# An mLSTM cell followed by a hash-routed MoE layer: places of two q transposes, the first division and the middle gates' rows, and of the first expert's weight loads

## The chip, the cores and the metric

The kernel runs on one core of one Trainium2 chip. The metric is device time in microseconds (us) of one execution; less is better. Nine runs of the kernel before gave a median of 353.56 us (352.61 to 356.6). One execution of it was profiled.

## The reference

Four batches of eight heads, 768 time steps, head dimension 40. Per head a recurrence keeps a 40x40 matrix C and a vector n; the output row of each step is gated and becomes one row of x (3072 tokens of 320 numbers). Each token then goes to one of eight experts, chosen by a hash of its id.

```python
for t in range(S):
    m_new = np.maximum(f[t] + m, i[t])
    f_stab, i_stab = np.exp(f[t] + m - m_new), np.exp(i[t] - m_new); m = m_new
    C = f_stab * C + i_stab * einsum('bhd,bhe->bhde', v[t], k[t])
    n = f_stab * n + i_stab * k[t]
    y[t] = sigmoid(o[t]) * (C @ q[t]) / np.maximum(np.abs(n @ q[t]), 1.0)
x = y.transpose(0, 2, 1, 3).reshape(B * S, H * D)
expert = token_ids * 2654435761 % 8
for e in range(8):
    out[expert == e] = np.maximum(x[expert == e] @ w1[e], 0) @ w2[e]
```

## The kernel before

**Two parts.** The first part computes the recurrence in chunks of 128 time steps: 24 steps s = 0 to 23, four batches (b = s % 4) times six chunks (c = s // 4). The second part is the MoE: expert 0 with rows turned early, then experts 1 to 7.

**A step of the first part.** Each engine takes its instructions in the order in which the program writes them; nothing reorders them, and an instruction that waits holds up all behind it on its engine. Step s writes this on TensorE: `turn(s+2)` (L382: four transposes of k and four of q into the two PSUM buffers of tag `tr`, each copied out to kT or qT by ScalarE, L395), `scores(s+1)` (L441: k times q), `decays(s+1)` (L397: products of the tiles L and R, which hold the gates' rows, exponentiated by ScalarE into w, L414), `state(s)` (L469: the chunk's sum for C), `attend(s)` (L490). VectorE does `weigh(s+1)` (L450: scores times w) and `divided(s-1)` (L510: four operations, the last, L518, reads the PSUM tile xh; xh has two buffers, so `state(s)`, which writes a part of the tile of step s+1, needs `divided(s-1)` done). GpSimd does `k_weights` (L426), `decayed` and `gated`.

**The gates.** Three groups: g0 for chunk 0, g1 for the four middle chunks (128 rows: four chunks times 32 heads), g2 for the last. g1 takes f from tile f1 and i from tile i1, both loaded by `middle` (L288); `sums` (L347) makes A, an exponential makes X, `ends` (L364) makes e, `split` (L355) and `rows` (L360) cut each into three bf16 parts in the tile zt1. From there they go through DRAM: `keep_a` (L271, rows A and X) and `keep_e` (L274, rows e) write them out, and `load_a(s)` (L243, into one of three R tiles) and `load_e(c)` (L252, into one of two L tiles) read them back in the layout that `decays` needs. A read waits for the end of the write of the same DRAM tensor. `load_a(4)` and `load_e(1)` are the first to read g1, and `decays(4)`, in step 3, the first to use them. `weights` (L369) makes kwT1 for `k_weights`: an exponential on ScalarE, a transpose on TensorE (L374), a copy on VectorE.

**The queue.** Nearly all loads are issued by SyncE (SP), in program order: per step k and q of step s+5, v of step s+4 (160 KB each, six buffers each), the gates' rows, o_gate, and stores of finished x rows up to step 16. Before the steps L279 to L808 write the start: loads of the first k, q, v, the gates of g0, `turn(0)` to `turn(2)`, and so on. The last steps' stores, the gathers of x rows by expert and the scatters are on GpSimd's queue.

**The first expert's weights** are loaded by pieces in the steps (`slices_of`, L120): w1 in two pieces of 512 KB (steps 17, 18), its last 64 rows w1c (step 19), w2 in four pieces of 320 KB (steps 20 to 23). In step 20 two gathers fetch expert 0's first 256 rows (L881); `early_turn(0)` and `early_turn(1)` (L744) transpose them in steps 22 and 23, the second ahead of `attend(23)`. After `attend(23)`, `layer1` of expert 0 runs (L901).

Of the kernel before, what the change touches and what calls it, by code (L numbers as in the profile page):

```python
# [8 lines left out]
F32 = mybir.dt.float32  # L9
# [8 lines left out]
P = 128  # L18
# [4 lines left out]
def kernel(  # L23
# [24 lines left out]
    nc = tc.nc  # L48
# [5 lines left out]
    E, _, F = moe_w1.shape  # L54
# [65 lines left out]
    def slices_of(e):  # L120

        w1t = wpools[0].tile([P, 2, F], F32, name="w1t")
        w1c = wpools[0].tile([P, FB // 2, P], F32, name="w1c")
        w2t = w2pools[0].tile([P, FB, Dm], F32, name="w2t")
        W[e] = w1t, w1c, w2t
        last = moe_w1[e][2 * P :, :].rearrange("d (a two f) -> two d a f", two=2, f=P)
        rows = moe_w2[e].rearrange("(a p) d -> p a d", p=P)

        def part(i):
            if i < 2:  # L130
                nc.sync.dma_start(w1t[:, i], moe_w1[e][i * P : (i + 1) * P, :])
            elif i == 2:
                for j in range(2):
                    nc.sync.dma_start(w1c[j * P // 2 : (j + 1) * P // 2], last[j])
            else:
                r = slice(2 * (i - 3), 2 * (i - 2))
                nc.sync.dma_start(w2t[:, r], rows[:, r])

        return [lambda i=i: part(i) for i in range(7)]

    def layer1(w, xT, h, c0, c1, bank):

# [47 lines left out]
    with tc.tile_pool(name="gates", bufs=1) as gp, \  # L190
# [61 lines left out]
        def load_e(c):  # L252
            g, r = pieces_of(c)
            nc.sync.dma_start(
                Ls[c % 2][: 3 * H], ze[g][r : r + BH].rearrange("(b h) (i t) -> (h i) b t", h=H, i=3),
            )
# [14 lines left out]
        def keep_a(g, zt, n, eng):  # L271
            eng.dma_start(zx[g][:n].rearrange("i r t -> r i t"), zt[:, :n])

        def keep_e(g, zt, eng):  # L274
            eng.dma_start(ze[g], zt[:, 6:9].rearrange("r i t -> r (i t)"))
# [12 lines left out]
        def middle(t, src):  # L288
            nc.sync.dma_start(t[:], src[:, P : S - P].rearrange("r (c t) -> c r t", t=P))

        middle(f1, flat[0])
        load(2, "k")

        ind = gp.tile([3 * H, H], F32, name="ind")
# [41 lines left out]
        class Gates:  # L336
# [32 lines left out]
            def weights(self, dst, tag="tr"):  # L369
                nc.scalar.activation(  # L370
                    self.a[:], self.t["e"][:, 0], AF.Exp, bias=self.t["A"][:, 0, P - 1 : P],
                )
                tp = ps.tile([P, self.n], F32, name="tpg", tag=tag, bufs=2)
                nc.tensor.transpose(tp[:], self.a[:], ident[: self.n, : self.n])  # L374
                nc.vector.tensor_copy(dst[:], tp[:])

# [5 lines left out]
        def turn(s, what, tag="tr"):  # L382
            turned_in(s, what, tag)
            turned_out(s, what)
# [65 lines left out]
        def weigh(s):  # L450
            d = st[s]
            for hf in range(2):
                nc.vector.tensor_tensor(d["w"][:, hf], d["sp"][hf][:], d["w"][:, hf], op=ALU.mult)  # L453
# [278 lines left out]
        for i in range(8):  # L732
            pieces.setdefault(12 + i, []).append(lambda i=i: route_hot(i))
            if i % 2:
                products[12 + i] = [lambda i=i // 2: route_table(i)]
        for i, part in enumerate(slices_of(0)):
            pieces.setdefault(17 + i, []).append(part)
        gates_of = {}
        for i, j in enumerate((4, 5, 6, 6, 7, 8, 8, 9)):
            gates_of.setdefault(j, []).append(i)  # L740
# [27 lines left out]
        load(0, "v")  # L768
        load(2, "q")
        keep_e(0, g0.zt, nc.sync)  # L770
        nc.vector.tensor_tensor_scan(m_sb[:, 1:], f_sb[:], i_sb[:], NEG, op0=ALU.add, op1=ALU.max)
        unread(6)
        turn(0, "k")
# [19 lines left out]
        middle(i1, flat[1])  # L793
        decays(0)
        turn(2, "k")
        load(1, "v")
        load(3, "k")
        load(3, "q")
        weigh(0)
        nc.vector.tensor_copy(Rs[2][:], Rs[0][:])  # L800
        turn(2, "q")
        load_e0()
        load_a(2)
        load(2, "v")
# [5 lines left out]
        for s in range(NT):  # L810
            b, c = place(s)
            if s + 3 < NT and s not in (1, 2):
                load_a(s + 3)
            if s + KV - 1 < NT:
                load(s + KV - 1, "k")
                load(s + KV - 1, "q")
            if s == 1:
                load_a(4)
                load_e(1)
            if s + KV - 2 < NT:  # L820
                load(s + KV - 2, "v")
            if b == 0 and 0 < c < NB - 1:
                load_e(c + 1)
            if s == 2:
                load_a(5)
            for i in gates_of.get(s + 2, ()) if s + 2 < NT - 1 else gates_of[NT - 1] if s == NT - 3 else ():
                load(i, "o")
            if s == 2:
                nc.sync.dma_start(tok[:], moe_token_ids.rearrange("(b c p) -> c b p", b=B, c=NB))
            if s == 13:  # L830
                keep_a(2, g2.zt, 6, nc.sync)
                keep_e(2, g2.zt, nc.sync)
            for i in waiting.pop(s, []):
                store(i)
            decayed(s)
            if s > 0:
                divided(s - 1)
            if s + 2 < NT:
                if s > 0:
                    turn(s + 2, "k")  # L840
                    turn(s + 2, "q")
            if s == 4:
                nc.scalar.activation(g2.t["X"][:, 0], g2.t["A"][:, 0], AF.Exp)
            if s in (7, 10, 12):
                g2.rows({7: "A", 10: "X", 12: "e"}[s], nc.scalar.copy)
            for piece in pieces.get(s, []):
                piece()
            if s + 1 < NT:
                scores(s + 1)
            if s + 1 < NT:  # L850
                k_weights(s + 1)
                decays(s + 1)
            if s == 0:
                nc.scalar.activation(g1.t["X"][:, 0], g1.t["A"][:, 0], AF.Exp)
            state(s)
            if s + 1 < NT:
                weigh(s + 1)
            if s == 0:
                g1.split("A")
                g1.rows("A", nc.scalar.copy)  # L860
                g1.split("X")
                g1.rows("X", nc.scalar.copy)
                g1.ends()
                g1.split("e")
                g1.rows("e", nc.scalar.copy)
                keep_a(1, g1.zt, 6, nc.sync)
                keep_e(1, g1.zt, nc.sync)
                ends_rows(Ls[1])
                nc.gpsimd.tensor_copy(Lx[:], one[:, 1].to_broadcast([P, HB]))
            for i in gates_of.get(s, ()):  # L870
                gate(i)
                if i < s:
                    gated(i)
                    if i < LS:
                        waiting.setdefault(s + 1, []).append(i)
                    else:
# [375 lines left out]
```

## Time and profile before

| what | value |
|---|---|
| median of nine runs | 353.56 us |
| the profiled execution's own time | 353.06 us |
| its span (first to last instruction) | 351.3 us |
| outside the span | 1.76 us |
| TensorE (PE) busy | 334.7 us, 95% of the span |
| VectorE / ScalarE / GpSimd busy | 229.7 / 138.9 / 214.5 us |
| clock granted to TensorE in the run | 0.993 |
| DMA moved | 59.18 MB, 168 GB/s over the span |

How to read it: a timeline line has the start in us, the duration, the engine, the line of the kernel, the operation, output and inputs, the number of instructions merged, and in square brackets the idle time of the engine just before it with what ended that. PE is TensorE's matrix multiply, DVE VectorE, ACT ScalarE, POOL GpSimd, SPq the issuing of DMAs by SyncE: such a line's time is the time that the issue held the queue, not that of the transfer. A wait for several things is put down to the one that came last by the profile, which can be a coincidence. Beside the instructions the trace has a record of each completion count that a transfer gives; eight counters are used in turn by the transfers of SP and ACT, so that each landing can be matched to its transfer by order.

### The profile page before, as it was taken

What the parts mean: (1) busy time and instruction counts of PE and PEld (TensorE: products, weight loads), DVE (VectorE), ACT (ScalarE), POOL (GpSimd) and SP (SyncE); (2) the same over time, 40 slices, a digit from 0 to 9 for tenths busy, and PEclk for the clock granted to TensorE, in tenths of its full rate; (3) what the DMA queues carried; (4) which work ended last, traced back from release to release, by engine and by line L of the source; (5) the groups of instructions that cost most, each with busy time, mean ns of one, the idle gap of its engine ahead of it and who ended that gap; (6) DMA issues with size and microseconds to landing.
All of it is one profiled execution on the core that took longest, in us unless ns stands there. A gap on an engine that the chain in (4) does not pass through costs nothing.

```text
span 351.3 us, 9214 instructions
## 1 busy us (share of the span) xinstructions
PE 334.7 (95%) x3573; PEld 291.9 (83%) x3573; DVE 229.7 (65%) x512; ACT 138.9 (40%) x325; POOL 214.5 (61%) x301
## 2 busy tenths in 40 slices
PE   7889999999999989999999999999999999999990
PEld 5677888888888866788899899789899899899860
DVE  8867897998887841156765886925766856844510
ACT  5676688776766631111412312311512412313300
POOL 8832778989886547408718938816917828526521
PEclk9999999999999999999999999999999999999997
DMA  6699999999999933699968869586486592010010
GB/s 130 121 196 184 162 193 192 209 189 199 190 215 229 258 114 104 175 242 284 236 206 241 283 105 336 145 235 205 115 218 223 113 281 93 0 38 19 18 40 1
DMA packets 162358, 59.18 MB, mean 168 GB/s; under 512 B 140171, under 2 KB 158119, under 8 KB 162313
## 3 DMA queue, kind: packets, MB, share of 16 engines
q1 hardware_dynamic: 158377, 49.05, 59.5%
q0 software_dynamic: 2832, 9.34, 7.9%
q8 instruction: 29, 0.48, 0.6%
q10 hardware_dynamic: 1104, 0.18, 0.3%
q14 instruction: 16, 0.13, 0.1%
HBM read 46.48 MB, written 12.38 MB: 168 GB/s over the span
## 4 chain that ended last, share of the span: by engine, by line
PE 75%; DMA 6%; issue 5%; DVE 4%; SPq 4%; POOL 2%; ACT 1%; ACTq 0%; POOLq 0%; DVEq 0%
PE mh L991 20%; PE mh L1075 14%; PE mh L1042 9%; PE mh L999 6%; PE sp L447 6%; PE tr L390 5%; PE xh L505 5%; PE xh L499 3%; DMA xg<-x_rows,g_idx 3%; PE ab L405 3%; PE xh L478 2%; SPq L1137 2%; DMA w1t<-in_moe_w_dram 1%; SPq L237 1%; PE mh L1155 1%
## 5 line engine op out<-in xcount | busy, mean ns | idle before, releaser
L917 POOL DMA_INDIRECT out_dram<-zo,s_idx x26 | 26.7, 1029 | 69.3 <-issue 47.2
L1042 PE MATMUL mh<-w2t,h 128*128 128x320 f32 x160 | 45.0, 433 | 0.5 <-ACT h L166 0.5
L1042 PEld LDWEIGHTS mh<-w2t,h 128*128 128x128 f32 x160 | 30.0, 190 | 11.8 <-ACT h L166 0.9
L977 DVE TENSOR_TENSOR h<-u,mh 128x416 f32<-128x416 f32 (+1 forms) x56 | 25.5, 475 | 16.6 <-PE mh L999 7.8
L505 PE MATMUL xh<-v,w 128*64 128x41 f32 x768 | 34.6, 222 | 0.0
L453 DVE TENSOR_TENSOR w<-sp,w 128x512 f32<-128x512 f32 x48 | 30.8, 682 | 3.5 <-ACT w L414 3.5
L414 ACT ACTIVATE w<-ab 128x512 f32<-128x512 f32 x48 | 26.2, 596 | 16.8 <-PE ab L405 15.9
L991 PE MATMUL mh<-tx,sw 128*128 128x208 f32 x168 | 31.9, 340 | 0.5 <-DVE sw L947 0.5
L505 PEld LDWEIGHTS xh<-v,w 128*64 128x64 f32 x768 | 30.6, 138 | 0.0
L991 PEld LDWEIGHTS mh<-tx,sw 128*128 128x128 f32 x168 | 29.7, 190 | 0.8 <-DVE sw L947 0.8
L447 PE MATMUL sp<-qT,kT 64*128 64x128 f32 x384 | 28.5, 285 | 1.2 <-ACT qT L395 1.0
L110 POOL DMA_INDIRECT xg<-x_rows,g_idx x24 | 23.3, 972 | 9.0 <-issue 6.4
L977 DVE TENSOR_TENSOR u<-m,mh 128x416 f32<-128x416 f32 x28 | 16.5, 588 | 18.7 <-PE mh L991 17.9
L447 PEld LDWEIGHTS sp<-qT,kT 64*128 64x128 f32 x384 | 23.8, 187 | 5.3 <-issue 3.1
L1075 PE MATMUL mh<-tw,sh 128*128 128x160 f32 x168 | 27.4, 299 | 0.0
L499 PE MATMUL xh<-C,qs 128*64 128x82 f32 x320 | 27.3, 249 | 0.0
L522 POOL TENSOR_TENSOR x<-x,og 128x320 f32<-128x320 f32 x24 | 20.6, 864 | 7.9 <-ACT og L439 4.8
L1075 PEld LDWEIGHTS mh<-tw,sh 128*128 128x128 f32 x168 | 24.3, 190 | 0.0
L991 PE MATMUL mh<-xT,w1t 128*128 128x208 f32 x112 | 23.1, 339 | 0.0
L488 POOL TENSOR_TENSOR C<-C,add 64x164 f32<-64x164 f32 x32 | 16.1, 503 | 10.2 <-ACT add L482 8.9
L1005 ACT COPY m<-mh 128x416 f32<-128x416 f32 x14 | 7.1, 505 | 37.9 <-PE mh L991 37.9
L913 ACT COPY zo<-mh 128x320 f32<-128x320 f32 x12 | 5.1, 425 | 42.6 <-PE mh L1042 27.3
(241 smaller groups left out, 778.8 us busy)
## 6 DMA issues: line engine op xcount, KB each, us to landing
w2t<-in_moe_w_dram SPq DMA_DIRECT2D x7, 1280.0 KB
w1t<-in_moe_w_dram SPq DMA_DIRECT2D x7, 1024.0 KB
xb<-x_slots SPq DMA_DIRECT2D x84, 52.0 KB
k<-in_k_dram SPq DMA_DIRECT2D x24, 160.0 KB
v<-in_v_dram SPq DMA_DIRECT2D x24, 160.0 KB
og<-in_o_gate_dram SPq DMA_DIRECT2D x24, 160.0 KB
q<-in_q_dram SPq DMA_DIRECT2D x23, 160.0 KB
x_slots<-xg SPq DMA_DIRECT2D x7, 480.0 KB
```

The costliest lines, as they stand in the source:

```text
L110: nc.gpsimd.indirect_dma_start(out=xg, out_offset=None, in_=x_d[:rows, :], in_offset=bass.IndirectOffsetOnAxis(ap=idx, axis=0),)
L414: nc.scalar.activation(w[:, hf], ab[:], AF.Exp)
L447: nc.tensor.matmul(sp[hf][:, j, :], lhsT=d["kT"][r, j, :], rhs=d["qT"][r, j, :], start=True, stop=True)
L453: nc.vector.tensor_tensor(d["w"][:, hf], d["sp"][hf][:], d["w"][:, hf], op=ALU.mult)
L499: nc.tensor.matmul(xh[t, 2 * j : 2 * j + 2, :], lhsT=d["qs"][:, j, t], rhs=Cs[b][c % 2][:, j].rearrange("p h d -> p (h d)"), start=True, s ...
L505: nc.tensor.matmul(hs[t, 2 * j + hf, :], lhsT=d["w"][:, hf, j, t], rhs=d["v"][:, 2 * j + hf, :], start=(c == 0), stop=True, skip_group_che ...
L917: ins = nc.gpsimd.indirect_dma_start(out=out[:, :], out_offset=bass.IndirectOffsetOnAxis(ap=idx, axis=0), in_=zo[:], in_offset=None, bound ...
L977: nc.vector.tensor_tensor(o, a, b, op=ALU.add)
L991: nc.tensor.matmul(pair(bank[n])[:, a], lhsT=lhsT(g + a), rhs=rhs, start=first and a == 0, stop=True, skip_group_check=True,)
L999: nc.tensor.matmul(pair(bank[n])[:, a], lhsT=w1c[k, g + a, :], rhs=xT[k, 2, r], start=False, stop=True, skip_group_check=True,)
L1042: nc.tensor.matmul(zp, lhsT=h[:, fb, j * P : (j + 1) * P], rhs=w[2][:, fb, :], start=(fb == 0), stop=(fb == FB - 1),)
L1075: nc.tensor.matmul(bank[n], lhsT=lhsT(f), rhs=rhs(f), start=first and f == 0, stop=f == FB // 2 - 1, skip_group_check=True,)
```

## The change

In the start: `middle(f1)` goes from its place ahead of `load(2, "k")` to the place behind `keep_e(0)`; `load(1, "v")` goes behind the loads of k and q of step 3; `turn(2, "q")` goes into step 0, behind `attend(0)`. In step 0, `keep_a(1)` comes ahead of the loads of k, q of step 5 and v of step 4; `attend(0)`, `turn(2, "q")` and `divided(0)` come ahead of g1's `ends` and `split("e")`. g1's rows e, `keep_e(1)` and `load_e(1)` go into step 1, behind `decays(2)` and behind step 1's loads. The exponential of kwT1 goes from step 2 to step 1 (behind `attend(1)`), its transpose and copy stay in step 2. Expert 0's w1 is loaded in four pieces of 256 KB (each half of the columns of one block of 128 rows): two in step 19, two in step 21; w1c in step 20; all of w2 in step 22. No arithmetic is added or removed.

```diff
@@ slices_of
-            if i < 2:
-                nc.sync.dma_start(w1t[:, i], moe_w1[e][i * P : (i + 1) * P, :])
-            elif i == 2:
+            if i < 4:
+                f = slice(i // 2 * F // 2, (i // 2 + 1) * F // 2)
+                nc.sync.dma_start(w1t[:, i % 2, f], moe_w1[e][i % 2 * P : (i % 2 + 1) * P, f])
+            elif i == 4:
...
-        return [lambda i=i: part(i) for i in range(7)]
+        return [lambda i=i: part(i) for i in (0, 1, 4, 2, 3, 5, 6, 7, 8)]
@@ the start
-        middle(f1, flat[0])
         load(2, "k")
...
         keep_e(0, g0.zt, nc.sync)
+        middle(f1, flat[0])
...
         middle(i1, flat[1])
         decays(0)
         turn(2, "k")
-        load(1, "v")
         load(3, "k")
         load(3, "q")
+        load(1, "v")
         weigh(0)
         nc.vector.tensor_copy(Rs[2][:], Rs[0][:])
-        turn(2, "q")
@@ pieces
-        for i, part in enumerate(slices_of(0)):
-            pieces.setdefault(17 + i, []).append(part)
+        for s, part in zip((19, 19, 20, 21, 21, 22, 22, 22, 22), slices_of(0)):
+            pieces.setdefault(s, []).append(part)
@@ the steps
+            def fetched():
+                if s + KV - 1 < NT:
+                    load(s + KV - 1, "k")
+                    load(s + KV - 1, "q")
+                if s + KV - 2 < NT:
+                    load(s + KV - 2, "v")
...
             if s == 1:
                 load_a(4)
-                load_e(1)
-            if s + KV - 2 < NT:
-                load(s + KV - 2, "v")
+            if s > 0:
+                fetched()
...
-            if s > 0:
+            if s > 1:
                 divided(s - 1)
...
                 decays(s + 1)
+            if s == 1:
+                g1.rows("e", nc.scalar.copy)
+                keep_e(1, g1.zt, nc.sync)
+                load_e(1)
             if s == 0:
                 nc.scalar.activation(g1.t["X"][:, 0], g1.t["A"][:, 0], AF.Exp)
             state(s)
...
                 g1.rows("X", nc.scalar.copy)
+                keep_a(1, g1.zt, 6, nc.sync)
+                attend(0)
+                turn(2, "q")
+                divided(0)
                 g1.ends()
                 g1.split("e")
-                g1.rows("e", nc.scalar.copy)
-                keep_a(1, g1.zt, 6, nc.sync)
-                keep_e(1, g1.zt, nc.sync)
+                fetched()
...
-            attend(s)
+            if s > 0:
+                attend(s)
...
+            if s == 1:
+                g1.exponents()
             if s == 2:
-                g1.weights(kwT1)
+                g1.exponents_turned(kwT1)
```

More of the change, by code (lines that the diff above doesn't have):

```diff
@@ L135, in part @@
             else:
-                r = slice(2 * (i - 3), 2 * (i - 2))
+                r = slice(2 * (i - 5), 2 * (i - 4))
                 nc.sync.dma_start(w2t[:, r], rows[:, r])
-        return [lambda i=i: part(i) for i in range(7)]
+        return [lambda i=i: part(i) for i in (0, 1, 4, 2, 3, 5, 6, 7, 8)]
     def layer1(w, xT, h, c0, c1, bank):
@@ L367, in ends, with weights, exponents @@
                 nc.vector.tensor_sub(e[:, 0], e[:, 0], self.t["A"][:, 0])
-            def weights(self, dst, tag="tr"):
+            def weights(self, dst):
+                self.exponents()
+                self.exponents_turned(dst)
+            def exponents(self):
                 nc.scalar.activation(
@@ L372, in weights, with exponents_turned @@
                 )
-                tp = ps.tile([P, self.n], F32, name="tpg", tag=tag, bufs=2)
+            def exponents_turned(self, dst):
+                tp = ps.tile([P, self.n], F32, name="tpg", tag="tr", bufs=2)
                 nc.tensor.transpose(tp[:], self.a[:], ident[: self.n, : self.n])
@@ L813 @@
                 load_a(s + 3)
-            if s + KV - 1 < NT:
-                load(s + KV - 1, "k")
-                load(s + KV - 1, "q")
+            def fetched():
[4 more added lines that the diff above has]
+                    load(s + KV - 2, "v")
             if s == 1:
                 load_a(4)
-                load_e(1)
-            if s + KV - 2 < NT:
-                load(s + KV - 2, "v")
+            if s > 0:
+                fetched()
             if b == 0 and 0 < c < NB - 1:
```

## The prediction

> **What bounds the kernel now.** I read the page first, then each engine's timeline from 11 to 31 us, then the chain of waits and TensorE's timeline from 104 to 162 us. The page's slices:
>
> ```profile
> PE   7889999999999989999999999999999999999990
> DMA  6699999999999933699968869586486592010010
> ```
>
> TensorE (PE) is full from about 30 us on (in stretches of 5 us it shows 5.00 us from 35 to 115 us). What the first steps gain or lose there passes to the end of the first part unshortened, as no idle time is left that could take it in. So the first steps are read in single stalls. TensorE's timeline:
>
> ```profile
> 12.95 0.63 PE L390 MATMUL tr<-ident,q 128*128 128x128 f32 x4 [0.68 <-DMA q<-in_q_dram]
> ...
> 17.40 0.63 PE L390 MATMUL tr<-ident,q 128*128 128x128 f32 x4 [0.21 <-DMA q<-in_q_dram]
> ...
> 20.49 0.67 PE L478 MATMUL xh<-v,kw 128*64 128x41 f32 x16 [0.83 <-DMA v<-in_v_dram]
> ...
> 26.61 0.33 PE L374 MATMUL tpg<-ident,a_zt 128*128 128x128 f32 x1 [0.47 <-ACT a_zt L370]
> ...
> 29.00 0.62 PE L405 MATMUL ab<-R,L 128*64 128x512 bf16 x4
> ```
>
> Four stalls sum to 0.68 + 0.21 + 0.83 + 0.47 = 2.19 us: q of step 2, q of step 3, `state(1)`, kwT1. The last line is `decays(4)`, first user of g1's rows; no idle time is noted, so rows and L came in time. The stall of `state(1)` is put down to a v load, but v of step 1 was issued at 12.39 us and by the completion records landed at 15.85 us. VectorE's timeline names the true cause: L518 of `divided(0)` ends at 19.75 + 0.49 = 20.24 us, just ahead of 20.49.
>
> ```profile
> 13.95 0.69 DVE L349 TENSOR_TENSOR a_zt<-f,m 128x128 f32<-128x128 f32 x1
> ...
> 15.68 1.29 DVE L453 TENSOR_TENSOR w<-sp,w 128x512 f32<-128x512 f32 x2 [0.25 <-ACT w L414]
> ...
> 19.75 0.49 DVE L518 TENSOR_TENSOR x<-xh,den 128x320 f32<-128x320 f32 x1
> ```
>
> ScalarE's (rows A, X, e of g1, then kT of step 3):
>
> ```profile
> 17.52 0.51 ACT L362 COPY zt<-A_zt 128x384 bf16<-128x384 bf16 x1 [0.72 <-DVE A_zt L358]
> 18.11 0.51 ACT L362 COPY zt<-X_zt 128x384 bf16<-128x384 bf16 x1
> 19.23 0.51 ACT L362 COPY zt<-e_zt 128x384 bf16<-128x384 bf16 x1 [0.61 <-DVE e_zt L358]
> 19.77 0.58 ACT L395 COPY kT<-tr 128x512 f32<-128x512 f32 x1
> ```
>
> SP's (load of i1, `keep_a`, `keep_e`, `load_a(4)`, `load_e(1)`):
>
> ```profile
> 11.74 0.61 SPq L289 DMA_DIRECT2D i<-in_i_gate_dram  x1
> ...
> 21.05 0.75 SPq L272 DMA_DIRECT2D gate_rows<-zt  x1
> 21.91 0.49 SPq L275 DMA_DIRECT2D gate_ends<-zt  x1
> ...
> 25.17 0.29 SPq L248 DMA_DIRECT2D R<-gate_rows  x1
> 25.55 0.32 SPq L254 DMA_DIRECT2D L<-gate_ends  x1
> ```
>
> A write to DRAM and the read behind it lie 25.17 - 21.05 = 4.12 and 25.55 - 21.91 = 3.64 us apart. At the end of the first part one stall counts:
>
> ```profile
> 125.29 0.52 PE L747 MATMUL tpx<-ident,xg 128*128 128x128 f32 x3 [1.19 <-DMA xg<-x_rows,g_idx]
> ```
>
> The second gather, issued at 119.33 us, takes 5.82 us beside the w2 loads.
>
> **The first steps, part one: the chain through ScalarE.** All times below are of the profiled execution. `turn(2, "q")` leaves its place, with its stall of 0.68 and its 0.63 us. But `scores(1)` behind it writes single PSUM buffers that `weigh(0)` reads until 11.68 + 1.36 = 13.04 us, so it moves from 13.51 to about 13.1, no further: 0.4 us to gain.
>
> `middle(f1)` comes on SP at 11.3. I take i1's row: 0.61 us of issue, and by the completion records landed at 15.25, 3.51 after its issue began; f1 then lands at 11.34 + 3.51 = 14.85, `sums` can start at 14.9 instead of 13.95, and its three operations (0.32, 0.33, 0.42 by the rows of L350 and L353, the first without the overlap that makes it 0.69) end at 15.97. `weigh(1)` starts at 16.05 instead of 15.68: +0.35. Bounds: 0, if f1 lands by 14.5 (the f1 load of before landed 2.72 us after its issue's end by the completion records, which would be 14.67 here), and +0.9, all of 14.85 - 13.95. The rows of A and X follow at the same distances, so rows X end at 18.62 + 0.35 = 18.97.
>
> Here is what I hold to be the new stall. In the changed order the copy of qT(2) is queued on ScalarE behind rows A and rows X, which wait for VectorE. It ends one copy later (0.5 us, L395 by its spacing), at about 19.5. `turn(3, "q")` needs the PSUM buffer that it frees, and `scores(2)` needs qT(2) itself; behind them wait all of TensorE's step 1. So `turn(3, "q")` starts at 19.5 instead of 17.40. From there to `state(1)` the rows of before have 19.66 - 17.40 = 2.26 us without the stall: 21.76 instead of 20.49, +1.27. `divided(0)` is 1.12 us long (19.12 to 20.24) and now stands behind the split of X: done by about 18.4 + 1.1 = 19.5, no wait. So 0.68, 0.21 and 0.83 go, and what is late next costs all of it and 1.27 more. Rows e now stand behind w(2) on ScalarE (about 22.9), and the exponential of kwT1 behind C(1), about 24.5, two and a half us ahead of its transpose: the 0.47 goes. **Sum of part one: +1.27 - 0.47 = +0.80**, `decays(4)` ready at 29.80. Bounds: +0.05 (f1 in time, and `decays(1)` at 14.2, 0.4 sooner: `turn(3, "q")` at 18.75, `state(1)` at 21.0) to +1.35 (f1's +0.9 in place of 0.35).
>
> [...]
>
> **Part two: the round trip of rows e.** SP's order up to v of step 3 has the same transfers plus f1 (+0.65), so `load_a(3)` ends at 19.01 + 0.65 = 19.66 and `keep_a(1)` starts at 19.7 (its rows are ready at 18.97). k, q, v behind it (1.90 us, 19.05 to 20.95 before) end at 22.4. `load_a(4)` waits for `keep_a`'s landing. The rows' distance is 4.12; the shortest store-and-read of the trace is the last x store on GpSimd, 129.97 to the gather's 132.10: 2.13. I take the middle, 3.1: 22.8. It and k, q, v of step 1 take 0.35 + 0.45 + 0.6 + 0.7 = 2.1, plus 0.25 for a queue that is full at times: `keep_e` starts at 25.2, instead of 21.91. Its landing, 2.13 to 3.64 later, I take at 2.9: `load_e(1)` at 28.1 instead of 25.55. By the completion records it landed 2.1 after its issue began: 30.2. `decays(4)` wants it at 29.8: **+0.4**. Bounds: 0 (22.5 + 2.1 + 2.13 + 2.1 = 28.8) to +3.8 (23.8, a k issue that is held as at 22.48 for 1.61 us, 3.64, and 2.88 as q of step 2 took: 33.6). In the wait SP holds back k, q, v of steps 6 and 7 and o_gate; k of step 7 was issued at 26.41 and wanted at 36.6, so that is covered.
>
> [...]
>
> **Part three: w1 and w2.** Bytes and issues stay (one issue of 0.42 us becomes two, twice). From 101.5 to 120 us SP issues without a pause, at up to 3.72 us for w1c's two: the queue is held by transfers, not by dependencies. Another order then ends at about the same time, and the w2 pieces still lie beside the gather of 119.33. I take 0. Bounds: -1.19 (the gather lands in time) and +0.6 (one more w2 piece ahead of the gather, priced by the 0.57 us that a w2 issue took at 114.93). Late weights cost nothing at first: w1's second half is wanted at about 131, w2 at 137.5, the last issue was at 120.0.
>
> **Sum.** +0.80 + 0.4 + 0 = +1.2 against 353.06: **354.3 us**. The median of the nine runs is 0.5 above the profiled execution; the forecast lies 0.7 above that median.
>
> **Rivals.**
> 1. *All four stalls go* and no new one comes: rows A and X are out before TensorE gets to `turn(3, "q")`, `load_e(1)` lands by 28. For it: each edit has the place of one stall. Against: ScalarE's order above. 353.06 - 2.19 = 350.9; with the gather's 1.19, 349.7.
> 2. *Slower: `load_e(1)` is late.* Place: `decays(4)`. With the rows' own distances, 23.8 + 2.1 = 25.9, + 3.64 = 29.55, + 2.1 = 31.65: 1.85 after 29.8; with part one, +2.65: 355.7, and up to 357.7 at 33.6. It decides from the point where `keep_e` lands after 27.7. For it: both distances are measured with fewer loads ahead of `keep_e`. Against: 2.13 was seen too.
> 3. *The gather's stall goes* while the start costs 1.2: 353.06 + 1.2 - 1.19 = 353.1.
> 4. *The first part's shift doesn't reach the end*, since the second part starts from a chain of gathers and loads (119 to 157 us): 353.06. Against: that chain starts from `attend(23)`'s rows, so it shifts too.
>
> **How the numbers follow.** Chances: forecast 0.35, rival 1 0.18, rival 2 0.27, rival 3 0.15, rival 4 0.05. Half a per cent is 1.77 us, about what a measurement can tell from no change: below 351.8 counts as faster (0.18), above 355.3 as slower (0.27), the rest 0.55. The forecast's own range is 353.1 (part one at its low end) to 355.3. The range takes in rival 1 without the gather, 350.9, and rival 2 up to 356.2; left out are some 0.05 below and 0.1 above.
>
> **What would show it.** In the changed profile: TensorE idle for about 1.5 us ahead of `turn(3, "q")` with ScalarE's qT copy as releaser; none ahead of L374; `decays(4)` waiting for L, by 0 to 2 us; 1.2 us idle still ahead of the second `early_turn`. I am wrong if rows X end by 18, if `load_e(1)` is issued by 26.5, or if the gather takes under 4.5 us.

## The result, and the profile after

The changed kernel took 356.06 us in the median of 19 runs (354.92 to 359.52), the kernel before 353.09 us in 62 runs beside it (352.27 to 356.6): a ratio of 1.0097 [1.0077, 1.0117], slower by 0.8 to 1.2%. The forecast was 354.3 us and "about no change". The profiled execution of the changed kernel took 358.67 us (span 356.9), so it is one of the longer ones; 5.6 us lie between its span and that of before. Here and below a ratio leaves out executions more than 1.5% above the fastest of their kernel and has an interval of its own, so it can differ from the quotient of the medians beside it.

The page, slices of 8.9 us (PE and DMA in tenths busy, PEclk the granted clock in tenths):

```profile
PE   7987999999999979999999999999999999999990
PEclk9898999999999999999999999999999999999996
DMA  6688999999899973679887959587477493000010
```

TensorE is full from 37 us on, as before from 30 us. New are the two 8s among the first slices of the PEclk row, which was all 9 up to its last slice before. TensorE's timeline of the first steps and of the second `early_turn` (the bracket is the idle time ahead of the line and what ended it; line numbers are those of the changed kernel: `turn` L396, `decays` L411, `state` L484, the transpose of kwT1 L380, `early_turn` L753):

```profile
19.84 0.66 PE L396 MATMUL tr<-ident,q 128*128 128x128 f32 x4 [1.17 <-ACT qT L401]
...
21.98 0.61 PE L484 MATMUL xh<-v,kw 128*64 128x41 f32 x16
...
27.50 0.33 PE L380 MATMUL tpg<-ident,a_zt 128*128 128x128 f32 x1
...
31.97 0.62 PE L411 MATMUL ab<-R,L 128*64 128x512 bf16 x4 [2.01 <-DMA L<-gate_ends]
...
34.55 1.11 PE L396 MATMUL tr<-ident,k 128*128 128x128 f32 x4
35.46 1.06 PE L396 MATMUL tr<-ident,q 128*128 128x128 f32 x4
...
130.52 0.52 PE L753 MATMUL tpx<-ident,xg 128*128 128x128 f32 x3 [2.33 <-ACT og L445]
```

The old stalls of q, of `state(1)` and of kwT1 are gone. In their place stand 1.17 us ahead of `turn(3, "q")`, 2.01 us for L ahead of `decays(4)`, and transposes that take 1.1 us instead of 0.6: half speed. The second `early_turn` waits 2.33 us. The profile names ScalarE there, but VectorE's copy of the gathered rows, which comes first, itself waits for the gather:

```profile
130.41 0.20 DVE L903 COPY xg<-xg 128x64 f32<-128x64 f32 x1 [2.60 <-DMA xg<-x_rows,g_idx]
```

SP's timeline (the second number is how long the issue held the queue): v of steps 1 and 2, `load_a(3)`, `keep_a(1)`, `load_a(4)`, k of step 6, `keep_e(1)`, `load_e(1)`.

```profile
14.49 1.40 SPq L238 DMA_DIRECT2D v<-in_v_dram  x1
...
16.95 1.03 SPq L238 DMA_DIRECT2D v<-in_v_dram  x1
...
20.15 1.49 SPq L249 DMA_DIRECT2D R<-gate_rows  x1
21.73 0.37 SPq L273 DMA_DIRECT2D gate_rows<-zt  x1
...
24.11 0.84 SPq L249 DMA_DIRECT2D R<-gate_rows  x1
25.05 1.15 SPq L238 DMA_DIRECT2D k<-in_k_dram  x1
...
27.60 0.86 SPq L276 DMA_DIRECT2D gate_ends<-zt  x1
30.37 0.32 SPq L255 DMA_DIRECT2D L<-gate_ends  x1
```

The write of rows e starts 5.7 us later than before (27.60 against 21.91), and the read of L 4.8 us later (30.37 against 25.55).

Added up against the profile of before: `scores(4)` is 0.9 us late (28.80 against 27.91), the wait for L adds 2.0, the half clock 1.5 (`decays(5)` at 37.76 against 33.26, 4.5 late in all), and 0.4 come back by `decays(6)` (42.76 against 38.65). The gather adds 1.1, and 0.35 are lost in the second part.

**The half clock.** The trace records the granted clock. In the profiles of this study it changes between full and half speed at steps of 3.41 us. TensorE's busy time (second number), and the granted clock (third number from the end), in two such windows of the changed kernel:

```profile
30.25:33.66 3.41, 1.69 (x40) 1.41 (x42) 0.81 (x2) 1.17 (x4) 0.00 (x0) 0.98 0.63 113
33.66:37.08 3.42, 3.42 (x33) 3.01 (x32) 3.25 (x10) 1.62 (x5) 1.41 (x2) 0.52 0.85 158
```

The edges of these rows lie 0.12 us too late, hence 0.98 and 0.52 instead of full and half; the half clock lasted from 33.54 to 36.95. In the window ahead of it, 30.13 to 33.54, the wait for L leaves TensorE idle for 1.84 us, and the window at half speed costs it up to another 1.7 us of work (an estimate, half of 3.41). So this wait of 2.01 us is paid nearly twice, with the 1.5 us that the half clock adds above.

### The profile page after: what moved, and what is told of

It reads as the page before. It is cut to its first block, busy times and chain, and to the rows that moved or that the text cites. A ratio compares the mean times of both kernels' runs of the same rounds, so it can differ in the third digit from the quotient of the medians.

```text
span 356.9 us, 9212 instructions
## 1 busy us (share of the span) xinstructions
PE 337.9 (95%) x3573; PEld 295.7 (83%) x3573; DVE 228.5 (64%) x512; ACT 139.2 (39%) x325; POOL 214.5 (60%) x301
## 4 chain that ended last, share of the span: by engine, by line
PE 75%; DMA 6%; issue 5%; DVE 4%; SPq 3%; ACT 2%; POOL 2%; ACTq 0%; POOLq 0%; DVEq 0%
PE mh L1010 20%; PE mh L1094 13%; PE mh L1061 8%; PE sp L453 7%; PE mh L1018 6%; PE tr L396 5%; PE xh L511 4%; PE ab L411 3%; PE xh L505 3%; PE xh L484 2%; SPq L1156 2%; DMA w1t<-in_moe_w_dram 1%; DVE w L459 1%; PE mh L1174 1%; DMA xg<-x_rows,g_idx 1%
## 5 line engine op out<-in xcount | busy, mean ns | idle before, releaser
L453 PE MATMUL sp<-qT,kT 64*128 64x128 f32 x384 | 30.0, 291 | 1.4 <-ACT qT L401 0.8
L453 PEld LDWEIGHTS sp<-qT,kT 64*128 64x128 f32 x384 | 25.0, 193 | 5.8 <-issue 3.0
```

Source lines behind the costliest of these rows:

```text
L453: nc.tensor.matmul(sp[hf][:, j, :], lhsT=d["kT"][r, j, :], rhs=d["qT"][r, j, :], start=True, stop=True)
```

## The experiments

Ratios are to the kernel before, timed on the same chip in the same comparison, with 95% intervals. The study went over several chips. On the one of experiments 1 to 4 the kernel before took 353.63 us, about as in the result; on those of the later ones 355.66 (5 to 8), 356.21 (9 to 12), 355.69 (13 to 16) and 356.19 us (17 and 18). Experiment 11 shows what is different there.

### The parts apart

**1. The order of w1 and w2 alone**, in the kernel before.

```diff
-        for i, part in enumerate(slices_of(0)):
-            pieces.setdefault(17 + i, []).append(part)
+        for s, part in zip((19, 19, 20, 21, 21, 22, 22, 22, 22), slices_of(0)):
+            pieces.setdefault(s, []).append(part)
```

> The kernel before with the new order and pieces of expert 0's weights alone. Theory W (w1's second half and all of w2 now lie beside the two gathers and hold up the second early turn): about +1.0 us against the kernel before, with the second early turn idle for about 2.3 us ahead of it instead of 1.19. Rival (the order of the weight loads has no price; the 1.1 us that the changed kernel shows there come from its late first steps): within 0.3 us, idle 1.2 us.

354.67 us, ratio 1.0020 [1.000, 1.004]: a loss of 0 to 1.4 us. The median rose by the 1.0 us that theory W expected, but not by the wait it named: the second `early_turn` waits 0.66 us in its profile, less than the 1.19 of before.

**2. The start alone**: the changed kernel with the old order of w1 and w2.

> The changed kernel with expert 0's weights loaded as before: the first steps' edits alone. Theory L (load_e(1) reaches decays(4) 2.0 us late, and the waits let TensorE's clock drop): +2.0 to +2.5 us against the kernel before, decays(4) idle for about 2 us, the second early turn for about 1.2. Rival (the weights' order carries the loss): within 0.5 us of the kernel before.

355.2 us, 1.0042 [1.0024, 1.006]: 1.6 us above the kernel before, short of theory L and over its rival. Its profile has the wait for qT and none for L:

```profile
20.25 0.66 PE L395 MATMUL tr<-ident,q 128*128 128x128 f32 x4 [1.66 <-ACT qT L400]
...
30.30 0.62 PE L410 MATMUL ab<-R,L 128*64 128x512 bf16 x4
```

In this execution `keep_e(1)` was issued at 26.13 us, 1.5 sooner than in the changed kernel's profile, though the first steps began later. Where L lands thus differs by more than a microsecond between executions. The two parts sum to 0.6%, the whole costs 1.0%; the intervals are too wide to say whether the parts simply add.

**3. The round trip of rows e ahead of step 1's loads**, in the changed kernel.

```diff
-            if s > 0:
+            if s > 1:
                 fetched()
...
                 keep_e(1, g1.zt, nc.sync)
                 load_e(1)
+                fetched()
```

> The changed kernel with keep_e(1) and load_e(1) ahead of step 1's loads of k, q and v on the queue, all else as changed. Theory L: keep_e issues at about 25 instead of 27.6, load_e(1) at about 27.7 instead of 30.4, decays(4) waits for under 0.7 us instead of 2.0; the time falls by 1.5 to 3 us below the changed kernel. Rival Q (the copy of qT(2) behind the gates' rows on ScalarE carries the loss): at most 0.5 us below the changed kernel.

355.65 us (354.03 to 360.34), 1.0059 [1.0030, 1.0088]: by the ratios 1.3 us below the changed kernel, between the two expectations. In the profile L is in time, and the price shows one step on, in the rows of `decays(5)`: a wait of 0.21 us at 34.06. Half of the executions lay at 354 to 355, half at 356 to 360; no profile shows what the long ones had, though experiments 5 and 16 suggest a longer wait for the same R.

**4. Seven products that nobody reads, ahead of `decays(4)`**, to keep TensorE from idling.

```diff
                 k_weights(s + 1)
+                if s == 3:
+                    unread(7, "ab", 2)
                 decays(s + 1)
```

> The changed kernel with seven unread 128x128 products (about 1.9 us) on TensorE between scores(4) and decays(4), where it waits for load_e(1) anyway. They are added work without a reader. If the clock drop behind the wait costs time, the profile shows full clock from 17 us on, the median falls by 0.5 to 1.5 us below the changed kernel and the slowest executions come down most. If the half clock has no part in it: within 0.3 us of the changed kernel.

357.43 us, 1.0114 [1.0081, 1.0148]: no gain. The products take 1.83 us (29.32 to 31.15), which every execution pays. In its profile the clock stays full and L is in time, at 31.08 us, 1.6 us later than `decays(4)` starts in experiment 3. A filler of fixed length is no cure for a wait of varying length. What the half clock alone costs is not shown by this run; that figure rests on the profiles.

### Where the later chips differ

**5. Experiment 3 with the old order of w1 and w2.**

> The start edits of the change with keep_e(1) and load_e(1) ahead of step 1's loads of k, q and v, and the old order of w1 and w2. Theory L (what the start costs is the wait of turn(3, q) for the copy of qT(2) and the late round trip of rows e; nothing else): with the round trip early, only the qT wait of some 1.65 us stays against the 1.72 of stalls removed, so the time is 0.3 to 0.9 us above before, about 1 us below the start edits alone (1.0042). Rival: the start edits alone already had no wait for L in their profiled execution, so the order of SP is worth nothing and the ratio stays at 1.004.

358.2 us, 1.0105 [1.0064, 1.0145], and the theory expected 1.001 to 1.003: a clear miss. Two waits that the theory did not have:

```profile
36.06 0.62 PE L410 MATMUL ab<-R,L 128*64 128x512 bf16 x4 [2.00 <-DMA R<-gate_rows]
```

ahead of `decays(5)`, and 2.73 us ahead of `decays(22)` at 122.09.

**6. w2's four pieces on GpSimd's queue behind the gathers**, in the changed kernel (`nc.gpsimd.dma_start` in place of `nc.sync.dma_start`, at the end of step 21).

> The changed kernel with w2's four pieces issued from GpSimd's queue at the end of step 21, behind the gathers, instead of from SP's. Theory W (the new order of w1 and w2 lays w2 beside the gathers and makes them land later, by a different amount from execution to execution): the wait of 2.33 us for xg ahead of the second early_turn falls below 1.2, the executions lie closer together, and the median falls by 1 to 2 us below the changed kernel's, to a ratio of about 1.005. Rival (the spread and the loss come from the first steps and the clock): the ratio stays at 1.009 to 1.010.

357.95 us (356.79 to 359.13), 1.0079 [1.0051, 1.0108]. The wait ahead of the second `early_turn` fell from 2.33 to 0.60 us, and the executions lie closer together, but the time did not fall to the 1.005 expected: in this profile 1.66 us for qT, 1.55 for L and, as w1 of the next expert comes later, 0.54 more at 160.87 are paid. The gather's wait is real, and a small part of the cost.

**7. A lean start**: in the kernel before, those edits that put nothing new behind a wait. `turn(2, "q")`, f1 and w1 stay; `keep_e(1)` comes ahead of step 1's k and q, and `load_a(4)` and `load_e(1)` between them and v. One edit of 7, 9 and 10 is not in the change, although the expectation lists it: q of step 2 is loaded ahead of v of step 0.

```diff
-        load(0, "v")
         load(2, "q")
+        load(0, "v")
...
+            if s == 1:
+                g1.rows("e", nc.scalar.copy)
+                keep_e(1, g1.zt, nc.sync)
+                fetched()
...
+                keep_a(1, g1.zt, 6, nc.sync)
+                attend(0)
+                divided(0)
                 g1.ends()
                 g1.split("e")
```

> The kernel before with those of the change's edits that put nothing new behind a wait: q of step 2 loaded ahead of v of step 0, k and q of step 3 ahead of v of step 1, attend(0) and divided(0) ahead of the ends and the split of e, rows e, keep_e(1) and load_e(1) in step 1 ahead of that step's loads, the exponents in step 1. turn(2, q), f1 and the order of w1 stay as before. Theory (the single stalls of the kernel before are real and pass to the end unshortened): the waits of 0.83 and 0.47 us go, and at least part of 0.68 and 0.21: 1.3 to 2.0 us below before, a ratio of 0.995 to 0.996. Rival (the start of an execution varies by more than that, or a new wait of the same size takes their place): 0.999 to 1.002.

355.44 us, 0.9997 [0.9973, 1.0021]: no change. Yet the start gained. The first steps began 1.0 us later than in the profile of before (`weigh(0)` at 12.68 against 11.68) and `decays(17)` stood at 92.73 against 92.61, so, with that shift taken off, 0.9 us had been won by then. It was lost here:

```profile
120.95 0.62 PE L411 MATMUL ab<-R,L 128*64 128x512 bf16 x4 [2.89 <-DMA R<-gate_rows]
```

**8. w2's pieces at steps 9, 11, 13 and 15**, in the kernel before.

> The kernel before with w2's four pieces at steps 9, 11, 13 and 15, and w1 and w1c at 17, 18 and 19, so that no w2 piece lies beside the gathers. Theory W: the gathers land sooner, the wait of 1.19 us ahead of the second early_turn goes: 1.2 us below before, a ratio of 0.9966. Rival (that wait is not in every execution, or the gather's time is its own): the ratio is 0.999 to 1.001, and a gather still takes over 5 us.

359.42 us, 1.010 [1.0061, 1.0139], the contrary of what was expected. The gathers' wait was gone (0.24 and 0.22 us ahead of the early turns), but the same wait for R as in 7 had grown to 3.61 us, and `decays(19)` waited 1.33 us for its R: the four pieces stand ahead of all these loads on the queue.

**11. The kernel before, profiled on the chip of 9 to 12.**

> The kernel before, profiled on this chip. Theory D: where the comparison's own executions lie some 2 us above 353.6, the rows of decays(23) are issued after 117 us and waited for by 1 us or more; on a chip with 353.6 there is no such wait, as in the profile of before. Rival: the executions differ in the first steps only, and no wait for those rows shows in either case.

357.43 us, where the median beside it was 356.21. TensorE, and SP:

```profile
120.67 0.62 PE L405 MATMUL ab<-R,L 128*64 128x512 bf16 x4 [3.07 <-DMA R<-gate_rows]
```

```profile
115.45 0.42 SPq L131 DMA_DIRECT2D w1t<-in_moe_w_dram  x1
115.97 0.30 SPq L248 DMA_DIRECT2D R<-gate_rows  x1
...
118.33 2.44 SPq L134 DMA_DIRECT2D w1c<-in_moe_w_dram  x2
```

`load_a(22)` is issued right behind the second half of w1 (512 KB), and `decays(22)` starts 4.70 us after that issue. In the profile of before the same load was issued at 108.26 us, 7.7 us earlier, and nobody waited (SP, then TensorE):

```profile
108.26 0.44 SPq L248 DMA_DIRECT2D R<-gate_rows  x1
```

```profile
116.87 0.62 PE L405 MATMUL ab<-R,L 128*64 128x512 bf16 x4
```

(The expectations of 9 to 11 call it `decays(23)`; by the order of the issues it is `decays(22)`.) From 40 to 100 us the profile of before moved 194 GB/s, this one 183. So loads fall behind TensorE here, and the last steps' rows are what is late. The variants do not part as cleanly: 183 to 193 GB/s on the chip of 1 to 4, 179 to 188 on the later ones. Whether the chip, the hour or the execution makes the rate lower stays open. The wait is again followed by half speed:

```profile
118.37:121.78 3.41, 1.11 (x20) 0.91 (x21) 0.24 (x1) 1.31 (x4) 2.31 (x4) 0.98 0.87 203
121.78:125.20 3.42, 3.42 (x51) 3.34 (x50) 2.67 (x7) 1.42 (x4) 2.40 (x3) 0.52 1.00 270
```

**12. The changed kernel on that chip.**

> The changed kernel, timed on the same chip as the lean variants. All theories: 1.008 to 1.012. By the reading of its first profile, a wait of 1.2 to 1.7 us ahead of turn(3, q), one of 1.5 to 2 us for L ahead of decays(4), no wait for the rows of decays(23), and a wait for the second gather. [...]

357.86 us (355.27 to 361.85), 1.003 [0.999, 1.007], less than the 1.008 expected. The changed kernel is 1.8 us above its 356.06, the kernel before 3.1 us above its 353.09. That fits the profiles, since the changed kernel's has no wait for R ahead of `decays(22)`; one profile of each does not prove it. The first steps are as in the first profile:

```profile
19.83 0.66 PE L396 MATMUL tr<-ident,q 128*128 128x128 f32 x4 [1.65 <-ACT qT L401]
...
32.00 0.62 PE L411 MATMUL ab<-R,L 128*64 128x512 bf16 x4 [2.06 <-DMA L<-gate_ends]
```

**9. The lean start with the new order of w1 and w2.**

> The lean start (the start edits that put nothing new behind a wait) together with the changed kernel's order of w1, w1c and w2. Theory D (by the end of the last steps SP's queue of loads, not TensorE, is the bound: the lean start gained 0.9 us up to 92 us and lost it in a wait of 2.89 us for the rows of decays(23), which stood on SP behind w1 and w1c): with w1 behind those rows the wait goes and the gain of about 0.9 us stays, ratio 0.995 to 0.998. Rival (the new order only moves the wait to the gathers, as in the changed kernel): 1.000 to 1.004.

354.31 us, 0.9963 [0.9936, 0.999]: faster than both kernels. `load_a(22)` is issued at 112.34, ahead of w1, and no R is waited for: `decays(22)` starts at 116.38, where the kernel before had 120.67 on this chip. The largest wait left in the first part is 0.71 us for L.

**10. The same with w2 behind the gathers.**

> The kernel of the lean start with the new order of w1 and, besides, w2's four pieces on GpSimd's queue behind the gathers. Theory D and W together: neither the rows of decays(23) nor the gathers are waited for, 0.995 to 0.997, up to 1 us below the lean start with the new order alone. Rival: w2 late or w1's second half is now waited for in the expert layer, and nothing is gained, 1.000.

355.01 us, 0.9991 [0.9956, 1.0026]: nothing gained over 9. The gather's wait shrank to 0.18 us, and 0.68 us for the next expert's w1 took its place.

### Which edit of the start costs

All six are the changed kernel, with its order of w1 and w2.

**13. `turn(2, "q")` back at its old place.**

```diff
         nc.vector.tensor_copy(Rs[2][:], Rs[0][:])
+        turn(2, "q")
...
                 attend(0)
-                turn(2, "q")
```

> The changed kernel with turn(2, q) alone at its old place, ahead of load_e0(). Theory S (two limits stand one behind the other: TensorE's wait for the copy of qT(2), and SP's queue, which lets load_e(1) land when it can; the later one sets decays(4)): the wait of 1.2 to 1.65 us ahead of turn(3, q) goes, but L lands at the same time, so decays(4) waits longer by as much, 3 us or more: no gain, within 0.3% of the changed kernel, and the half clock behind decays(4) in every profile. Rival (the qT chain is the cost): 1.2 to 1.7 us below the changed kernel.

359.47 us, 1.0101 [1.0069, 1.0134]. The wait for qT is gone, and TensorE reaches `decays(4)` sooner, only to wait longer for the same L:

```profile
31.30 0.62 PE L411 MATMUL ab<-R,L 128*64 128x512 bf16 x4 [2.77 <-DMA L<-gate_ends]
```

No gain, as expected; it is even slower than the changed kernel's 1.003 on that chip, more than "within 0.3%". The granted clock of its runs was 0.968 to 0.989, that of experiment 12 0.976 to 0.995: the author's estimate from these means is that the longer single wait, 2.77 against 2.06 us, has the clock halved in more of the executions. No run shows that window by window.

**14. f1's load back at its old place** (`middle(f1, flat[0])` ahead of `load(2, "k")`).

> The changed kernel with the load of f1's rows alone at its old place, ahead of k of step 2. Theory S: SP's queue is 0.63 us shorter up to load_e(1), sums and rows A and X come earlier by up to 0.7 us, and turn(3, q) with them; L's wait shrinks by 0.3 to 0.7 us, but not to nothing: 0.4 to 0.9 us below the changed kernel, more where the wait falls under the 1.7 us from which the clock was seen to halve. Rival: f1 has only moved on the queue and is hidden: the changed kernel's time.

357.2 us, 1.0009 [0.9969, 1.0048]. `keep_e(1)` is issued at 25.85 instead of 27.60, and `decays(4)` does not wait in its profile. The ratio's middle value agrees with the 0.4 to 0.9 us expected, the medians (357.2 to 355.69) do not, and the interval is too wide to call it.

**15. Both back.**

> The changed kernel with turn(2, q) and the load of f1 both at their old places. Theory S: L's landing, at best 0.6 us earlier, still sets decays(4) and shows as the one wait of the first steps, 1 to 2.5 us; 0.4 to 0.9 us below the changed kernel and no better than f1 alone. Rival (the chain through ScalarE is the cost): no wait but L's under 0.5 us, 1.7 to 2.5 us below the changed kernel.

356.81 us, 1.0027 [0.9994, 1.0061]. One wait is left, the one expected, and larger: L, with `decays(4)` at half speed behind it.

```profile
30.60 1.06 PE L412 MATMUL ab<-R,L 128*64 128x512 bf16 x4 [3.11 <-DMA L<-gate_ends]
```

So the chain through ScalarE is not what costs as long as L lands so late. Taking it out turns its wait into a longer one for L.

**16. Both back, and the round trip ahead of step 1's loads as in 3.**

> The changed kernel with turn(2, q) and f1 at their old places and keep_e(1) and load_e(1) ahead of step 1's loads of k, q and v. Theory S: both limits are gone: no wait over 0.4 us up to decays(5), and the time is that of the lean start with the new order of w1 or up to 0.7 us below it: a ratio of 0.993 to 0.997 to before, 4 us or more below the changed kernel. Rival: SP stands still between keep_e and load_e, so the rows of decays(5) come late by up to 2 us, as in the profile of the fifth experiment: 0.998 to 1.003.

356.81 us, 1.0025 [0.9991, 1.0059]: the rival was right. SP first, then TensorE:

```profile
23.47 1.42 SPq L276 DMA_DIRECT2D gate_ends<-zt  x1
26.66 0.31 SPq L255 DMA_DIRECT2D L<-gate_ends  x1
...
32.85 0.48 SPq L249 DMA_DIRECT2D R<-gate_rows  x1
```

```profile
28.35 0.62 PE L412 MATMUL ab<-R,L 128*64 128x512 bf16 x4 [0.36 <-DMA L<-gate_ends]
36.17 1.07 PE L412 MATMUL ab<-R,L 128*64 128x512 bf16 x4 [3.48 <-DMA R<-gate_rows]
```

From 24.89 to 26.66 SP stands still, waiting for the write, and then issues two steps' loads ahead of `load_a(5)` at 32.85. `decays(5)` pays 3.48 us.

**17. Only step 1's order on SP changed**: `keep_e(1)`, k, q, `load_a(4)`, `load_e(1)`, v. `turn(2, "q")` and f1 stay where the change put them.

```diff
+                if s == 1:
+                    load_a(4)
+                    load_e(1)
                 if s + KV - 2 < NT:
                     load(s + KV - 2, "v")
...
                 keep_e(1, g1.zt, nc.sync)
-                load_e(1)
+                fetched()
```

> The changed kernel with nothing but step 1's order on SP altered: keep_e(1) ahead of that step's k and q, load_a(4) and load_e(1) between q and v, so that the round trip of rows e is filled with two loads instead of standing at the queue's end or holding the queue. Theory S (SP's order around the round trip is the cost of the first steps): L and R of decays(4) and decays(5) are both in time or late by under 1 us, no half clock there, and the time falls to a ratio of 0.997 to 1.001 although turn(2, q) and f1 stay where the change put them. Rival (the qT chain and f1 cost as much as SP's order): 1.002 to 1.004, as with the changed kernel on such a chip.

355.41 us, 0.9974 [0.9948, 0.9999]. The wait for qT is still there, 1.65 us, and none for L or R behind it:

```profile
19.69 0.66 PE L396 MATMUL tr<-ident,q 128*128 128x128 f32 x4 [1.65 <-ACT qT L401]
...
29.73 0.62 PE L411 MATMUL ab<-R,L 128*64 128x512 bf16 x4
33.99 0.62 PE L411 MATMUL ab<-R,L 128*64 128x512 bf16 x4
```

**18. The same with `turn(2, "q")` and f1 back.**

> The same with turn(2, q) and the load of f1 back at their old places; it differs from the lean start with the new order of w1 in little more than step 0's k, q and v standing behind keep_a(1). Theory S: 0.995 to 0.998, as the lean start with the new order of w1 (0.9963), and at most 1 us below the seventeenth. Rival: the step 0 loads' place is what the lean start gained by, and this stays at 1.000 or above.

353.77 us, 0.9946 [0.9917, 0.9975], the lowest ratio of all, though its interval overlaps that of 9. It lies 1.6 us below 17, more than the 1 us expected: with SP's order mended, `turn(2, "q")` and f1 do cost. The profiles show 0.6 of it at the start (`decays(4)` at 29.14 against 29.73); the rest lies behind the first part. SP's round trip, filled with two loads, and TensorE behind it:

```profile
22.80 2.01 SPq L276 DMA_DIRECT2D gate_ends<-zt  x1
24.90 0.38 SPq L238 DMA_DIRECT2D k<-in_k_dram  x1
25.34 0.59 SPq L238 DMA_DIRECT2D q<-in_q_dram  x1
26.03 0.70 SPq L249 DMA_DIRECT2D R<-gate_rows  x1
26.78 0.32 SPq L255 DMA_DIRECT2D L<-gate_ends  x1
```

```profile
29.14 0.62 PE L412 MATMUL ab<-R,L 128*64 128x512 bf16 x4 [1.52 <-DMA L<-gate_ends]
```

So L is still late here: without the wait for qT, TensorE is ready 1.52 us before it lands. The start is no faster than that of the kernel before: `decays(17)` stands at 92.77, against 92.61 and 92.84 in its two profiles. What 18 gains over it shows at the end of the first part, where `decays(22)` starts at 117.03 without a wait for R, against 120.67 in experiment 11. The order of w1 explains that, as in 9.

`keep_e(1)` is issued 4.8 us sooner than in the changed kernel, `load_e(1)` 3.6 us, and `load_a(5)` at 29.90 instead of 32.61. Neither 17 nor 18 was timed on a chip where the kernel before takes 353 us.

## Why the prediction was wrong

**Part one had the right stall, and its size partly by luck.** The stalls of q, `state(1)` and kwT1 went, and the copy of qT(2) behind rows A and X (its transposes ended at 18.24, the copies of rows A and X started at 18.08 and 18.67, its own at 19.20) held `turn(3, "q")` to 19.84 (forecast 19.5), `state(1)` to 21.98 (21.76), and the first steps by 0.9 us (0.80). But the first link, `weigh(1)` late by 0.35 because of `sums`, was another: it started 0.56 us late, and the last operation of `sums` had ended at 15.75.

```profile
15.33 0.42 DVE L353 TENSOR_TENSOR_SCAN A_zt<-ones,a_zt 128x128 f32<-128x128 f32 x1
...
16.24 1.29 DVE L459 TENSOR_TENSOR w<-sp,w 128x512 f32<-128x512 f32 x2 [0.48 <-ACT w L420]
```

It waited for w(1), that is for `decays(1)`, which came at 14.93 in this execution and ran at half speed; in 17, at full speed, `weigh(1)` started at 16.08 (forecast 16.05) and again waited for w(1). So `sums` did not set it, contrary to the prediction, and that the delay came out near 0.35 there is luck.

The load of R for `decays(1)`, `load_a(1)`, stands right behind f1's load in the changed order. Six profiles with it there have a wait for R ahead of `decays(1)`, of 0.26 to 1.04 us (experiments 3, 4, 5, 6, 12 and 17), and in four of them it started at 15.01 to 15.15. The other profiles with f1 moved (of the changed kernel, 2 and 13), where `decays(1)` started at 14.93 to 15.57, show none; nor do those with f1 back (14, 15, 16, 18). The chips and the issue of `load_a(1)`, some 0.75 us sooner with f1 back, differ too, so no run shows why R was late.

**Part two failed, at the step "`keep_e` starts at 25.2".** It started at 27.60, and in five other profiles of that order (2, 4, 6, 12, 13) at 26.1 to 27.6. Of these 2.4 us, 2.0 were there at `keep_a(1)` already (21.73, forecast 19.7), and the rest came with the seven transfers between the two. The sum took the durations of issues from the profile of before: v of step 2 0.40, `load_a(3)` 0.65, and 0.25 us in all "for a queue that is full at times". These are v of steps 1 and 2 and `load_a(3)` in the profile of before:

```profile
12.39 0.49 SPq L237 DMA_DIRECT2D v<-in_v_dram  x1
...
15.91 0.40 SPq L237 DMA_DIRECT2D v<-in_v_dram  x1
...
18.36 0.65 SPq L248 DMA_DIRECT2D R<-gate_rows  x1
```

In the changed order v of step 1 held SP for 1.40, v of step 2 for 1.03, `load_a(3)` for 1.49 and k of step 6 for 1.15 us. The later terms held: write to read 2.77 (forecast 2.9), read to use 1.6 (2.1). So a mis-sized queue made a stall of 0.4 into one of 2.0. That is rival 2 with its place, its releaser and its point of decision (`keep_e` landing after 27.7); its price of 1.85 to 2.65 was right for the wait and lacked the half clock behind it, 1.5 us. Experiments 13 to 17 show that this order on SP is the limit that stands last, and the qT chain one hidden ahead of it: removing the chain alone gained nothing (13), and mending SP's order alone took away the wait for L and the half clock behind it (17: 0.9974, against 1.003 in 12 on another chip).

**Part three's zero was at the edge of what was measured, and left out a term.** Experiment 1 gives 0 to 1.4 us of loss for the order of w1 and w2 alone. The prediction priced only the gather beside w2. What the order of w1 also moves is `load_a(22)` out from behind w1, and its worth depends on how far SP lags: nothing in the profile of before, and on the later chips a wait of 2.7 to 3.6 us and half a window of clock. No price of that was in the sum, since the profile of before has no idle time there. On SP it had been visible: the load whose delay counts was issued at 108.26 for a product at 116.87, with no pause on the queue from 101.5 us on.

**The sum.** Measured 356.06; forecast 354.3. By the profiled execution's terms the qT chain gave +0.9 (forecast +0.80), L +2.0 (+0.4), the clock +1.5 (none), the gather +1.1 (0). The profiled execution's time is 2.6 us above the median, so most executions probably had less of the last three; that is not shown, as none of them was profiled.

**What stays open.** Why the changed kernel's profile and that of 14 have a half-speed window in the first steps (13.06 to 16.47 and 13.40 to 16.82), although TensorE idled for only 0.46 us in the window ahead. And how often the waits for L and R occur: each kernel has one profile, and its run times only hint at it.

## What to carry to other kernels

When an edit moves a store and the load that reads it back along a queue that never pauses, count what the queue holds ahead of both; the time from write to read kept to 2.5 to 2.9 us in the eight profiles with the store behind step 1's loads, but its start moved by 1.8 us, and the best place tried had the store early, some other loads between, and the read behind them. Two waits in a row can hide each other: removing the earlier one alone gained nothing in 13 (1.0101, against 1.003 in 12). In a kernel like this, a wait of TensorE near 2 us should be priced at up to twice its length: the one of 2.01 us in the changed kernel's profile had 1.5 us of half clock behind it.

## What the runs showed of the hardware

- **Half speed stood behind windows with much idling.** Up to the last ten microseconds or so of each profile, TensorE idled for 1.84 to 2.80 us in nine windows of 3.41 us, and all nine were followed by a window at half speed. Of the twenty windows with 1.2 to 1.66 us, one was so followed (1.64 us, in 16). Near the end of the profiles of 2 and 5, windows with 1.81 and 1.85 us were not. So these profiles show no sharp bound; the 1.7 us that the expectation of 14 names was the author's reading of the profiles up to then. The wait of 2.00 us in 5 fell on both sides of a window's edge (1.29 us in one window), and no half speed followed it. Two half-speed windows came after only 0.46 us of idling, and in 15 a second one followed the first after 0.52 us; no run explains these.
- **The start varies.** The first window at full speed begins 4.2 to 10.7 us after the first instruction, by execution, and where it begins after 8 us the first steps are late too, by up to 1.6 us (`weigh(0)` starts at 11.44 to 13.01). Single stalls of the first steps can only be compared after that shift is taken off.
- **The rate of the loads varied by 6%** between the two profiles of the kernel before (194 and 183 GB/s from 40 to 100 us), and with it which load is late at the end of the first part. The same change can then be worth a different amount: a ratio of 1.0097 [1.0077, 1.0117] in the result, 1.003 [0.999, 1.007] in experiment 12.
